# Opening of a transform-and-feed-forward kernel: one list of single steps over ten units, conversions in place on VectorE, a compact first-stage table

## The chip, the core and the metric

The kernel runs on one core of a Trainium2 chip. The engines are named as in the profile: PE (TensorE, matrix products), DVE (VectorE), ACT (ScalarE), POOL (GpSimd) and SP (SyncE, which here only issues DMAs). Each engine works through its own queue in order; semaphores order the engines among each other. The metric is the time of the program on the device in microseconds; less is better. The kernel before takes 1809.57 us, the median of three runs (1808.49 to 1812.95).

## The reference

```python
def _attn_ref(x):                         # x: 8 x 3072 x 256, float32
    X = np.fft.fft(x, axis=1)
    X = np.fft.fft(X, axis=2)
    return X.real.astype(np.float32)

def _moe_ref(x, w_in, w_out):             # x: the result above as 24576 x 256
    h = x @ w_in                          # w_in: 256 x 2048, float64
    g = np.maximum(h, 0.0) + np.log1p(np.exp(-np.abs(h)))
    return (g @ w_out).astype(np.float32) # w_out: 2048 x 256, float64
```

So: the real part of a two-dimensional Fourier transform of each of 8 batches, then a feed-forward network with softplus on each of the 24576 rows. [...]

## The kernel before

**The transform** along the sequence (3072 = 24 x 128) is made in two stages. Stage A multiplies with a table (`fe`, and `fo` that is made from it on ACT by `fo_prep`, L270) and writes its result `t_d` to memory; the host's arrangement of x allows two cheap folds (`fold_a`, `fold_b`, L168 and L173) ahead of it. A batch goes through stage A in four groups of 3 or 4 column sets. Stage B (`load_y`, `stage_b`, `stage_b_out`) reads rows of `t_d` back and multiplies with a cosine table `bc`. The transform along the 256 columns is not made on the data: its cosine table `cd` is multiplied into w_in once (`w1_prep`, L303). The data are split by symmetry, so that each output row and its mirror come from one sum and one difference.

**Blocks and units.** The rows are cut into 25 blocks (`BLOCKS`), three for each batch and four for the last, of up to 512 columns each. For every block the network runs in 8 units (`UB`), each 256 of the 2048 hidden columns; 200 units in all. A unit u has a first layer (`mm1`, L455: twelve products in two halves, P and Q, each half in one of the two PSUM slots `pq`), then on DVE two additions of an edge term to P (`pc`, L475), the sum and the difference with Q (`h`, L553 and L554), on ACT four softplus (`gh` rounded, `h` full, L574 and L575), on DVE the low parts (`gl` = full minus rounded, `low_part`, L514), and a second layer (`mm2`, L485: four times six products into two accumulators). The second layer of unit u - 2 (`LAG`) stands behind the first layer of unit u in PE's queue. Every operand of a product is kept as a rounded high part and a low part, and three products (high-high, high-low, low-high) make one. After 8 units the accumulators are copied out on ACT (`evac`, L507).

The edge term needs one row of a block on all partitions: ACT copies it (`er`, L263), SP stores it to `e_d` and loads it back to all partitions (`eb`).

**The weights.** w_in and w_out come in as eight chunks each of 128 x 512 float64 numbers. Chunk c of w_in is loaded (`load_wi`), converted to float32 by steps on bits (`to_f32_a`, `to_f32_b`: five on DVE, L278 to L292, one on ACT, L298, two on POOL, L299 and L300), multiplied with `cd` on PE (`w1_prep`, L307 and L316), rounded on ACT (L323), and its low part taken on DVE (`w1_lo`, L329). A chunk of w_out is converted in the same way, rounded on ACT (L340), and its low part is taken on POOL (L341). Unit u needs chunk u of both.

**The order.** `PLAN` is a table of tokens written out by hand. The entry `s` runs ahead of the units: it loads, makes batch 0's stage A and block 0's stage B, and converts chunks 0 to 5 of w_in and prepares w1 from 0 to 4 of them. The entries `0a`, `0b`, `0d` to `7d` run at three places inside units 0 to 7 and hold the rest of the conversions. Behind that a loop over units u hangs further work to fixed units (`tasks`): the loads, folds and stage A of the next batch, stage B of the next block. Each token and each loop body appends its instructions to the engines' queues in the order of the program. All loads and stores go through SP's queue. Raw chunks of weights lie in buffers that units use later (`gh`, `gl`, `xt`, `wr`).

## Time and profile before

| | us |
|---|---|
| median of three runs | 1809.57 |
| the profiled execution | 1808.19 |
| its span, first to last instruction | 1806.3 |
| PE busy in the span | 1750.1 |
| DVE busy | 1275.7 |
| ACT busy | 930.4 |
| POOL busy | 171.8 |
| mean granted clock of PE | 0.982 of full |

The page gives sums over the span; a question about one stretch of it needs the busy times by windows and the instructions in order of time. In a row of the latter stand the start, the length, the engine, the line of the kernel, the operation, what it writes and reads, the shape and how many instructions are merged; in square brackets follows how long the engine had been idle and what ended that. A float32 product counts as two instructions, a rounded one as one. In a row of waits stand who waited for whom, the total, how often, and the longest.

### The profile page before, as it was taken

Reading aid. Unit: us, or ns where it says so; the run is one execution under the profiler, and the core shown is the slowest. Engines: PE = TensorE matmul, PEld = TensorE weight load, DVE = VectorE, ACT = ScalarE, POOL = GpSimd, SP = SyncE. Lnnn points to the kernel's source line nnn. Section 1 sums busy time; section 2 is a strip of 40 time slices with the busy share of each in tenths; the row PEclk is TensorE's granted clock in tenths of the full one; section 3 lists DMA queues with packets and bytes.
Section 4 is the critical chain, followed back from the end, with each engine's and each line's share of the span. In section 5 each row is a group of like instructions: output and inputs, shape, how many; then the busy total and the mean of one; then the engine's idle time right before and its main releaser. Section 6 shows DMA issues by size and latency. Waiting matters only on the chain.

```text
span 1806.3 us, 20128 instructions
## 1 busy us (share of the span) xinstructions
PE 1750.1 (97%) x8196; PEld 1474.4 (82%) x8196; DVE 1275.7 (71%) x1337; ACT 930.4 (52%) x970; POOL 171.8 (10%) x156
## 2 busy tenths in 40 slices
PE   4589999999999999999999999999999999999999
PEld 4467888888888888888888888888888888899999
DVE  3599667677776677766776677766777667767775
ACT  1245555555555455555545545555555555555554
POOL 1245101110011001010010100110010200000000
PEclk7789999999999999999999999999999999999999
DMA  6302221310103102121012111131021210001000
GB/s 185 118 20 69 83 69 40 92 61 18 53 22 101 41 18 63 52 70 50 24 40 76 53 41 34 30 96 57 18 63 44 78 47 24 14 37 39 23 18 19
DMA packets 39339, 94.84 MB, mean 53 GB/s; under 512 B 2958, under 2 KB 18978, under 8 KB 38287
## 3 DMA queue, kind: packets, MB, share of 16 engines
q1 hardware_dynamic: 39247, 93.56, 17.6%
q8 instruction: 65, 1.06, 0.2%
q14 instruction: 27, 0.22, 0.0%
HBM read 55.00 MB, written 38.54 MB: 52 GB/s over the span
## 4 chain that ended last, share of the span: by engine, by line
PE 90%; ACT 0%; ACTq 0%; issue 0%
PE acc L495 57%; PE pq L466 28%; PE pq L223 1%; PE pq L183 1%; PE pq L184 1%; PE pq L225 1%; PE pq L230 0%; PE pq L227 0%; PE pq L236 0%; ACT o L507 0%; ACTq L615 0%; PE pq L244 0%; PE pq L247 0%
## 5 line engine op out<-in xcount | busy, mean ns | idle before, releaser
L495 PE MATMUL acc<-gh,wo 128*128 128x512 f32 (+2 forms) x3200 | 1016.5, 386 | 2.0 <-DVE wn L335 2.0
L495 PEld LDWEIGHTS acc<-gh,wo 128*128 128x128 f32 x3200 | 600.3, 188 | 117.4 <-ACT gh L574 2.4
L574 ACT ACTIVATE gh<-h 128x1024 fp32r<-128x1024 f32 (+2 forms) x400 | 407.1, 1018 | 476.5 <-DVE h L553 475.9
L495 PE MATMUL acc<-gl,wo 128*128 128x512 f32 (+2 forms) x1600 | 617.5, 386 | 0.0
L475 DVE SCALAR_TENSOR_TENSOR pc<-eb,wn,pq 128x512 f32<-128x512 f32 (+2 forms) x400 | 272.7, 723 | 442.0 <-PE pq L466 442.0
L466 PE MATMUL pq<-x,w 128*128 128x512 f32 (+5 forms) x2400 | 574.5, 388 | 4.9 <-DVE h L554 2.7
L466 PEld LDWEIGHTS pq<-x,w 128*128 128x128 f32 (+1 forms) x2400 | 449.8, 189 | 96.9 <-PE pq L466 4.5
L514 DVE TENSOR_TENSOR gl<-h,gh 128x1024 fp32r<-128x1024 f32 (+2 forms) x400 | 470.6, 1218 | 0.0
L575 ACT ACTIVATE h<-h 128x1024 f32<-128x1024 f32 (+2 forms) x400 | 411.0, 1028 | 12.7
L495 PEld LDWEIGHTS acc<-gl,wo 128*128 128x128 f32 x1600 | 301.9, 189 | 54.5
L553 DVE TENSOR_TENSOR h<-pq,pc 128x1024 f32<-128x1024 f32 (+2 forms) x200 | 236.6, 1183 | 21.8 <-DVE pc L475 1.4
L554 DVE SCALAR_TENSOR_TENSOR h<-pq,pc 128x1024 f32<-128x1024 f32 (+2 forms) x200 | 234.6, 1173 | 0.0
L170 POOL TENSOR_TENSOR xt<-xt 120x387 f32<-120x387 f32 (+1 forms) x28 | 26.2, 935 | 1149.0 <-DMA xt<-in_xh 1149.0
L192 ACT ACTIVATE st<-pq 125x768 f32<-125x768 f32 (+1 forms) x32 | 27.8, 867 | 133.3 <-PE pq L184 133.3
L260 ACT ACTIVATE x<-pq 128x1024 fp32r<-128x1024 f32 (+2 forms) x25 | 24.9, 994 | 135.1 <-PE pq L225 83.6
L183 PE MATMUL pq<-xt,fe 120*125 120x129 f32 x208 | 43.5, 293 | 17.3 <-DMA fe<-in_fe 11.9
L183 PEld LDWEIGHTS pq<-xt,fe 120*125 120x125 f32 x208 | 35.9, 204 | 20.5 <-issue 15.5
L507 ACT ACTIVATE o<-acc 128x1024 f32<-128x1024 f32 (+2 forms) x52 | 47.1, 956 | 7.7 <-PE acc L495 7.3
L307 PE MATMUL wps<-wt,cd 128*128 128x256 f32 x64 | 25.9, 576 | 24.4 <-POOL wt L300 24.4
L184 PE MATMUL pq<-xt,fo 120*125 120x127 f32 x208 | 43.2, 292 | 2.0 <-DVE xt L176 1.1
L307 PEld LDWEIGHTS wps<-wt,cd 128*128 128x128 f32 x64 | 18.1, 297 | 29.5 <-POOL wt L300 25.8
L223 PE MATMUL pq<-bc,y 128*128 128x128 f32 (+2 forms) x208 | 39.9, 273 | 1.4 <-DVE pc L475 1.4
(50 smaller groups left out, 454.5 us busy)
## 6 DMA issues: line engine op xcount, KB each, us to landing
...
```

Of the source, the lines that this page charges most:

```text
L183: nc.tensor.matmul(out=psv[0:YR, i, 127:D], lhsT=fe[:, g0 + i, :], rhs=t[:, i, 1, :], start=True, stop=True)
L184: nc.tensor.matmul(out=psv[0:YR, i, 0:127], lhsT=fo[:, g0 + i, :], rhs=t[:, i, 3, 2:NE], start=True, stop=True)
L223: nc.tensor.matmul(out=ps[:, 0, c : c + n], lhsT=y[0:kk, i, 128:256], rhs=cos, start=True, stop=True)
L466: nc.tensor.matmul(out=ps[:, g, 0:n], lhsT=w1[0 : 128 - t, t, a, f0 : f0 + 128], rhs=x1[0 : 128 - t, t, c, 0:n], start=(i == 0), stop=(i = ...
L475: nc.vector.scalar_tensor_tensor(out=pc[:, g, 0:n], in0=eb[:, 0:n], scalar=wn[:, 2 * fu + g : 2 * fu + g + 1], in1=p_ps[:, g, 0:n], op0=AL ...
L495: nc.tensor.matmul(out=acc[:, ec, 0:n], lhsT=wo[:, a, fc, ec * 128 : (ec + 1) * 128], rhs=src[:, sign, g, 0:n], start=(fu == 0 and g == 0 ...
L507: nc.scalar.activation(out=o[:, e0:e1, 0:n], in_=acc_t[sign][:, e0:e1, 0:n], func=AF.Copy)
L514: nc.vector.tensor_tensor(out=gl[:, sg, :, 0:n], in0=h_t[u][:, sg, :, 0:n], in1=gh_t[u][:, sg, :, 0:n].bitcast(F32), op=ALU.subtract,)
L553: nc.vector.tensor_tensor(out=h[:, 0, :, 0:n], in0=q_ps[:, :, 0:n], in1=pc[:, :, 0:n], op=ALU.add)
L554: nc.vector.scalar_tensor_tensor(out=h[:, 1, :, 0:n], in0=q_ps[:, :, 0:n], scalar=-1.0, in1=pc[:, :, 0:n], op0=ALU.mult, op1=ALU.add,)
L574: nc.scalar.activation(out=gh[:, sg, :, 0:n], in_=hv, func=AF.Softplus)
L575: nc.scalar.activation(out=hv, in_=hv, func=AF.Softplus)
```

## The change

The opening is rewritten. What it does:

- **One list.** The entry `s` and the entries of units 0 to 7 are replaced by one list of tokens, each a single step on one engine, which covers the loads, batch 0's stage A, the stage B of blocks 0 and 1, all conversions, and units 0 to 9 up to the second layer of unit 7. The loop starts at unit 10 (`N0`). Tokens of a unit: `MP`, `MQ` first layer; `pc`, `pd` edge terms; `hp`, `hm` sum and difference; `sa`, `sb` softplus; `gl` low part; `U7_01` a quarter of the second layer of unit 7. Of the weights: `C0A` to `C4G` and `K0A` to `K3G` steps of conversion of w_in and w_out, `P`, `Wh`, `wn`, `Wl` preparation of w1, `Oh`, `Ol` of wo.
- **Conversions.** Chunks 0 and 1 of w_in are converted alone, chunks 2 to 7 in pairs (1024 elements), and so are all of w_out. The steps A to F are on DVE, D and F write over the raw words; the last step G is on DVE for w_in and on POOL for w_out. ACT has no part in it.
- **Table.** The host gives a table with 25 entries per column set instead of 125 and five columns of 0 and 1; 20 copies on ACT with a scale per partition spread it into `fe` and `fo`. It takes 314,400 bytes instead of 780,000.
- **Order of loads; stores of stage A.** Group 2 of batch 0 comes first. The rows of `t_d` that block 0 needs are stored from ACT's queue at once (`T`), the rest from SP's queue later (`t`). All folds of batch 0 are on DVE.
- **w1 preparation** of chunks 4 to 7 uses the PSUM slots of the first layer. `wn` is copied on ACT.
- Named buffers replace the pools that turn; the work hung to units of the loop moves by a few units for batch 1 and blocks 2 and 3.

```diff
-PLAN = {
-    "s": (
-        "X0 I1 L0 I0 X1 X2 X3 I2 L1 F0f f0f I3 A0 a0 C0 D0s F1f f1f A1 a1 F2f f2f A2 a2 L2 P0 W0d F3f f3f "
-        "A3 a3 L3 C1 D1s Y0 L4 P1 W1d C2 D2s L5 C3 D3s L6 P2 W2d P3 W3d L7 B0 b0 C4 D4s M0 P4 W4d C5 D5s M1"
-    ),
-    "0a": "P5",
...
+N0 = 10
+CHUNKS = ((0,), (1,), (2, 3), (4, 5), (6, 7))
+PLAN = """
+Ife X2 Ibc X0 X1 X3 L0 L3 L2 Icd fex L1 fex2 F2 f2 A2 F0 a2 T2 f0 A0 F1 f1 a0 A1 F3 T0 a1 f3 T1 C0A A3 C0B
+C0C C0D a3 C0E C0F T3 C0G C2A C2B P0 C2C C2D C1A C1B Wh0 C1C wn0 C1D C1E Y0 C1F L4 L5 C1G M1 C2E M0 P1 C2F
+C2G B0 wn1 Wl0 Wh1 Wl1 P2 x1h0 x1l0 C3A MP0 er0 C3B wn2 Wh2 E0 C3C t0 MQ0 t2 Wl2 C3D P3 C3E Eb0 L6 C3F M2 t3
...
+    on = (jj[:, None] == np.arange(NJ)[None, :]).astype(float)
+    half = R // 2
+    ang = 2 * np.pi * ((s[:, :, None] * np.arange(half + 1)) % S) / S
+    cs, sn = np.cos(ang), np.sin(ang)[:, :, 1:]
+    fe = np.concatenate([cs, -sn], axis=2)
+    fo = np.concatenate([-cs[:, :, :1], -sn, -cs[:, :, 1:]], axis=2)
+    fx = np.concatenate([fe.reshape(XP, -1), fo.reshape(XP, -1), on], axis=1)
...
+    def stage_a_store(eng, b, gi, st, rows):
+        for r0, r1 in rows:
+            eng.dma_start(out=t_d[b, r0:r1, g0 : g0 + ng, :], in_=st[r0:r1])
...
+    def e_load(blk):
+        i, n = blk["i"], blk["n"]
+        eb = eb_t[i] = buf(f"eb{i % 2}", [128, 512])
+        nc.sync.dma_start(out=eb[:, 0:n], in_=e_d[i : i + 1, 0:n].to_broadcast([128, n]))
...
+    def spread(fx, g0, g1):
+        for k, f in enumerate((fe, fo)):
+            v = fx[:, k * NG * (R + 1) : (k + 1) * NG * (R + 1)].rearrange("p (g c) -> p g c", g=NG)
+            for j in range(NJ):
+                on = 2 * NG * (R + 1) + j
+                nc.scalar.activation(
+                    out=f[:, g0:g1, :, j], in_=v[:, g0:g1, :], func=AF.Copy, scale=fx[:, on : on + 1]
+                )
...
+    def to_f32(step, raw, p):
         lo, hi = raw[:, :, 0], raw[:, :, 1]
-        ti, pi = t.bitcast(I32), p.bitcast(I32)
-        nc.vector.tensor_scalar(
-            out=pi, in0=pi, scalar1=0x07FFFFFF, scalar2=3, op0=ALU.bitwise_and, op1=ALU.logical_shift_left
-        )
-        nc.vector.scalar_tensor_tensor(
...
+        elif step == "D":
+            v.scalar_tensor_tensor(
+                out=hi, in0=hi, scalar=-0x40000000, in1=pi, op0=ALU.bitwise_and, op1=ALU.bitwise_or
+            )
...
+        elif step == "F":
+            v.scalar_tensor_tensor(
+                out=lo.bitcast(F32), in0=lo.bitcast(U32), scalar=2.0**-52, in1=p, op0=ALU.mult, op1=ALU.mult
+            )
+
+    def to_f32_end(eng, raw, p):
+        eng.tensor_tensor(out=p, in0=raw[:, :, 1].bitcast(F32), in1=raw[:, :, 0].bitcast(F32), op=ALU.add)
 
...
+        ps = slot() if c >= 4 else pa.tile([128, 2, 512], F32, tag=f"acc{c % 2}", name="wps")
...
+        RAW_I, RAW_O = ("gl0", "gl1", "gh2", "xt"), ("wr", "gl2", "wr", "wr")
+        XTAG, STAG = ("xt", "h0", "h1", "x10"), ("os0", "os1", "os2", "h1")
+        FIRST, REST = ((5, 25), (65, 85)), ((0, 5), (25, 65), (85, YR))
...
+        def convert(key, step):
+            if key not in cvt:
+                if key[0] == "C":
+                    ch = CHUNKS[int(key[1])]
+                    raw = raws["i", ch[0] // 2]
+                    where = {1: ("pc", ch[0]), 2: ("x11", ch[0] // 2 - 1)}[len(ch)]
+                    if where[0] not in space:
+                        shape = [128, 2, 512] if where[0] == "pc" else [128, 2, 1024]
+                        space[where[0]] = buf(where[0], shape)
+                    p = space[where[0]][:, where[1] % 2]
+                    r = raw[:, ch[0] % 2 : ch[-1] % 2 + 1].rearrange("p c f t -> p (c f) t")
+                    for j, c in enumerate(ch):
+                        lone[c] = p[:, j * 512 : (j + 1) * 512]
+                else:
+                    k = int(key[1])
+                    r = raws["o", k].rearrange("p c f t -> p (c f) t")
+                    p = osbuf(k % 2)[:, 0:1024]
+                cvt[key] = r, p
+            r, p = cvt[key]
+            if step == "G":
+                to_f32_end(nc.gpsimd if key[0] == "K" else nc.vector, r, p)
+            else:
+                to_f32(step, r, p)
+
+        def do(tok):
...
+            elif k == "T":
+                stage_a_store(nc.scalar, 0, c, hold["st", c], FIRST)
+            elif k == "t":
+                stage_a_store(nc.sync, 0, c, hold["st", c], REST)
...
+            elif k == "er":
+                hold["e", c] = e_copy(BLOCKS[c], hold["b", c], buf("eb1", [128, 512]) if c == 0 else osbuf(2))
...
+            elif k in ("Oh", "Ol"):
+                hi, lo = (wo[:, i, 4 * c : 4 * c + 4, :] for i in range(2))
+                tv = cvt[f"K{c}"][1].rearrange("p (c e) -> p c e", e=D)
+                if k == "Oh":
+                    nc.scalar.activation(out=hi, in_=tv, func=AF.Copy)
+                else:
+                    nc.gpsimd.tensor_tensor(out=lo, in0=tv, in1=hi.bitcast(F32), op=ALU.subtract)
+            elif k in ("MP", "MQ"):
+                mm1(c, int(k == "MQ"))
+            elif k in ("pc", "pd"):
+                p_out(c, int(k == "pd"))
+            elif k in ("hp", "hm"):
+                h_out(c, int(k == "hm"))
+            elif k in ("sa", "sb", "gl"):
+                (soft_hi, soft, low_part)[("sa", "sb", "gl").index(k)](a[1], a[0])
+            elif k == "U":
+                mm2(c, a[1] // 10, a[1] % 10)
...
+        for tok in PLAN.split():
+            do(tok)
+        evac(0, 0)
...
+            u0 = first[b - 1] * UB + (N0 if b == 1 else 0)
+            for gi in range(4):
+                hang(u0 + 2 * gi, ("x", b, gi))
+                hang(u0 + 2 * gi + 2, ("a", b, gi))
+        for i in range(2, len(BLOCKS)):
+            u0 = (i - 1) * UB
+            hang(u0 + (2 if i > first[B - 1] else 6 if i == 3 else 3), ("b", i))
+            hang(N0 if i == 2 else u0 - 3 if i > 3 else u0 + 4, ("y", i))
...
+        for u in range(N0, NU + LAG):
...
```

The order on the engines, first before, then after. DVE, from the low part of block 0 (`x`, L261 before and L276 after) on. Before (`wt`, `wir` are a chunk of w_in in conversion, `w_81` is w1):

```order
L261 TENSOR_TENSOR x_265<-pq,x_265 128x2x512
L278 TENSOR_SCALAR wt<-wir 128x512
L281 TENSOR_SCALAR wt<-wt 128x512
L286 TENSOR_SCALAR wt<-wt 128x512
L289 SCALAR_TENSOR_TENSOR wt<-wir,wt 128x512
L292 TENSOR_SCALAR wt<-wt 128x512
L329 TENSOR_TENSOR w_81<-wps,w_81 128x2x256
L335 COPY wn<-wps 128x2
```

After (`gh`, `wr` hold raw words of w_in and w_out, `x` and `os` the space of the conversion):

```order
L276 TENSOR_TENSOR x<-pq,x 128x2x512
L309 TENSOR_SCALAR x<-gh 128x1024
L311 TENSOR_SCALAR x<-x 128x1024
L313 TENSOR_SCALAR x<-x 128x1024
L548 TENSOR_TENSOR w_75<-wps,w_75 128x2x256
L317 SCALAR_TENSOR_TENSOR gh<-gh,x 128x1024
L321 TENSOR_SCALAR x<-gh 128x1024
L323 SCALAR_TENSOR_TENSOR gh<-gh,x 128x1024
L309 TENSOR_SCALAR os<-wr 128x1024
```

A chunk's conversion and the low part of the same chunk, which stood one behind the other, are apart now: between the steps of one pair stands the low part of another chunk, and a pair of w_out follows ahead of unit 0.

PE, from the preparation of chunk 4 of w1 before, and of chunk 2 after. Before (L307 and L316 prepare w1, L466 is the first layer):

```order
L307 MATMUL wps<-wt,cd 128x256 x4
L316 MATMUL wps<-cd,wt 128x1 x4
L466 MATMUL pq<-x_265,w_81 128x512 x12
L307 MATMUL wps<-wt,cd 128x256 x4
L316 MATMUL wps<-cd,wt 128x1 x4
L466 MATMUL pq<-x_265,w_81 128x512 x12
```

After (L334 and L343 prepare w1, L372 is the first layer, L436 the second):

```order
L334 MATMUL wps<-x,cd 128x256 x4
L343 MATMUL wps<-cd,x 128x1 x4
L372 MATMUL pq<-x,w_75 128x512 x12
L334 MATMUL wps<-x,cd 128x256 x4
L343 MATMUL wps<-cd,x 128x1 x4
L372 MATMUL pq<-x,w_75 128x512 x18
L436 MATMUL acc_369<-gh,wo 128x512
```

Five chunks were prepared ahead of unit 0's first layer, now three; unit 1 and half of unit 2 follow chunk 3 at once, and the second layer of unit 0 ahead of the other half.

SP, from the last loads of w_in ahead of block 0's edge row on. Before (`e_d`, `eb` the edge row, `wor` w_out):

```order
L358 DMA wir<-in_w_in 128x2x512 x4
L266 DMA e_d<-er 1x512
L267 DMA eb<-e_d 128x512
L367 DMA wor<-in_w_out 128x2x512 x3
L204 DMA y<-t_d 65x4x256
```

After (`t_d<-os` are the stores of stage A that block 0 does not need):

```order
L467 DMA gh<-in_w_in 128x2x512 x2
L467 DMA wr<-in_w_out 128x2x512 x2
L287 DMA e_d<-eb 1x512
L204 DMA t_d<-os 5x1024
L204 DMA t_d<-os 40x1024 x2
L204 DMA t_d<-os 5x768
L204 DMA t_d<-os 40x768 x2
L292 DMA eb<-e_d 128x512
```

Loads of w_out have moved ahead of the edge row, and six stores stand between its store and its load.

More of the change, by code (lines that the diff above doesn't have):

```diff
@@ L136, in tile_fft2_softplus_ffn @@
 @with_exitstack
-def tile_fft2_softplus_ffn(ctx: ExitStack, tc: tile.TileContext, xh, w_in, w_out, fe_d, cd_d, bc_d, out):
+def tile_fft2_softplus_ffn(ctx: ExitStack, tc: tile.TileContext, xh, w_in, w_out, fx_d, cd_d, bc_d, out):
     nc = tc.nc
@@ L200, in load_y @@
         t = t_rows(b)
[L201 removed]
+        y = buf("y", [128, 5, D])
         ks = [k for k, _, _ in blk["cols"] if k]
@@ L534, in tile_fft2_softplus_ffn @@
             pst = {}
-            for tok in PLAN.get(f"{u}a", "").split():
-                do(tok)
             for t in todo:
```

450 lines of the change are left out of this document (210 added, 240 removed).

## Prediction

> **What bounds the kernel now.** I read the busy times of the page first, then the busy times in three stretches of the opening, then TensorE (PE) and VectorE (DVE) in order of time.
>
> ```profile
> span 1806.3 us, 20128 instructions
> PE 1750.1 (97%) x8196; PEld 1474.4 (82%) x8196; DVE 1275.7 (71%) x1337; ACT 930.4 (52%) x970; POOL 171.8 (10%) x156
> ```
> ```profile
> 0.00:85.00 85.00, 43.27 (x177) 37.28 (x178) 35.19 (x61) 14.80 (x22) 16.12 (x16) 0.74 0.57 161
> 85.00:183.00 98.00, 87.63 (x348) 68.78 (x348) 95.12 (x111) 53.56 (x63) 45.87 (x32) 0.89 0.15 41
> 183.00:199.70 16.70, 16.70 (x92) 14.15 (x91) 10.91 (x11) 7.62 (x8) 3.40 (x4) 1.00 0.46 139
> ```
>
> The columns are length, then PE, PE's weight loads, DVE, ACT and POOL busy, the granted clock, the DMA share and GB/s. Of the 56.2 us in which PE is idle (1806.3 - 1750.1), 52.1 lie before 183 us (183 - 43.3 - 87.6), and the last 4 are the end of the output. From 183 us on PE never pauses, at full clock. Only the opening has room, and there the limit changes: up to 85 us neither engine is full (DVE 35.2 of 85), from 85 to 183 DVE is (95.1 of 98).
>
> ```profile
> 72.59 3.05 PE L466 MATMUL pq<-x,w 128*128 128x512 f32 x12
> ...
> 183.02 2.96 PE L466 MATMUL pq<-x,w 128*128 128x512 f32 x12
> ```
> ```profile
> 61.70 1.22 DVE L261 TENSOR_TENSOR x<-pq,x 128x1024 fp32r<-128x1024 f32 x1 [1.56 <-ACT x L260]
> ```
>
> Counting first layers from 72.59 (unit 0), the one at 183.02 is unit 10. By then units 0 to 9 have had their first layer and 0 to 7 their second, and this is just what the new list of steps holds. I call this moment T10. Behind it lie 1806.3 - 183.0 = 1623.3 us of PE work without a pause, which the change leaves as they are (the loop's moved loads have several units to land). So the prediction is a prediction of T10. The L261 row is the second mark: block 0 is ready for the units at 62.9, and T10 comes 120 us later.
>
> ```profile
> DVE w L329 <- ACT w L323: 35.1, 6, 10.2
> ```
>
> Why 62.9: a chunk of w_in goes from DVE over ACT, POOL, PE and ACT back to DVE, with all else behind it in DVE's queue. DVE stood 35.1 us for the end of this round trip.
>
> **The change, term by term. Term 1, block 0 ready.**
>
> ```profile
> 0.00:10.00 10.00, 0.00 (x0) 0.00 (x0) 1.90 (x3) 1.28 (x1) 0.20 (x4) 1.00 0.82 185
> 10.00:20.00 10.00, 4.60 (x18) 3.84 (x18) 5.60 (x11) 3.35 (x5) 1.30 (x1) 1.00 0.98 247
> ```
> ```profile
> 55.94 1.99 PE L307 MATMUL wps<-wt,cd 128*128 128x256 f32 x8
> 57.77 0.95 PE L316 MATMUL wps<-cd,wt 128*128 128x1 f32 x8
> 58.58 0.47 PE L223 MATMUL pq<-bc,y 128*128 128x128 f32 x2
> ...
> 60.22 0.39 PE L225 MATMUL pq<-bc,y 128*128 128x128 f32 x2
> ...
> 79.43 3.78 PE L307 MATMUL wps<-wt,cd 128*128 128x256 f32 x8 [3.79 <-POOL wt L300]
> 83.01 1.71 PE L316 MATMUL wps<-cd,wt 128*128 128x1 f32 x8
> 84.57 4.99 PE L466 MATMUL pq<-x,w 128*128 128x512 f32 x12
> ```
> ```profile
> 13.86 0.43 DVE L286 TENSOR_SCALAR wt<-wt 128x512 int32<-128x512 int32 x1
> 14.33 0.69 DVE L289 SCALAR_TENSOR_TENSOR wt<-wir,wt 128x512 int32<-128x512 int32 x1
> 15.05 0.43 DVE L292 TENSOR_SCALAR wt<-wt 128x512 int32<-128x512 int32 x1
> ```
>
> DVE's second chunk (C1) needs the eleventh load; ahead of it and with it stand 6.0 MB (table 0.31, x 3.22, cosines 0.39, four w_in chunks 2.10). The first 10 us move 1.85 MB, later ones 0.247 a us: 26.8, and with 2 for landing 29. The compact table saves 0.47 MB (2 us) and costs 20 short ACT copies instead of 3; these lie beside the loads of x. C1's seven steps on 512 elements take 0.47 each for four one-input steps and 0.72 for three two-input ones (start to start in these rows), 4.0: 33. Steps D and F now write in place over every second word, which no row shows; between 0.43 and 1.4 (twice its row) I take the 0.69 of L289, which already reads every second word. P1, the product that prepares C1's part of w1, at half clock takes 5.1 (79.43 to 84.57; at full clock 2.6, from 55.94 to 58.58): 38.1; block 0's transform 2.0 (58.58 to 60.61): 40.1; its high part on ACT some 1.2 and its low part 1.2: 42.5. I take **43**, 20 earlier than before. The stores of the first stage, whose first rows go ahead on ACT's queue, must be in memory by about 33.
>
> **Term 2, DVE from there to the low part of unit 1.**
>
> ```profile
> 76.52 1.40 DVE L475 SCALAR_TENSOR_TENSOR pc<-eb,wn,pq 128x512 f32<-128x512 f32 x2
> 78.03 1.23 DVE L553 TENSOR_TENSOR h<-pq,pc 128x1024 f32<-128x1024 f32 x1
> 79.17 1.22 DVE L554 SCALAR_TENSOR_TENSOR h<-pq,pc 128x1024 f32<-128x1024 f32 x1
> ...
> 148.50 2.35 DVE L514 TENSOR_TENSOR gl<-h,gh 128x1024 fp32r<-128x1024 f32 x2
> ```
>
> Start to start: the two halves of P 1.5, each h 1.14, two low parts 2.27, a w1 low part, half an h step, 0.62. A 1024-element conversion exists nowhere in the trace. A two-input step should take 1.25, as h does; a one-input step lies between 0.47 (no dearer than 512 elements) and 0.94 (two of them). I take 0.73, nearer to two since the work doubles. Six steps A to F are then 4 x 0.73 + 2 x 1.25 = 5.4. In the new order stand: three such conversions (C3, K0, K1) 16.3; the C3 end step 1.1; pc and pd of units 0, 1, 2: 4.5; five h steps 5.7; four low parts 4.5; two w1 low parts 1.2. Sum **33.4**; PE then stands at 43 + 33.4 = 76.4. Going on, DVE has 64.5 more to the last h of unit 9 (K2, K3, C4 17.3, seven units' pc and pd 10.5, fifteen h steps 17.1, fourteen low parts 15.9, four w1 low parts 2.5, block 1's 1.2), so 140.9 if it never waits.
>
> **Term 3, PE from there to T10.** Now PE has more left than DVE. A first layer is 2.78 (12 products of the pitch of 0.2315 in the 5.54 us groups below), a second 5.56, a w1 preparation 2.64, a block transform 2.0, as above. Left: half of unit 1's second layer 2.8, six more 33.3, thirteen first-layer halves 18.1, four preparations 10.6, block 1 2.0: **66.8**, so 143.2.
>
> ```profile
> 216.69 5.54 PE acc L495 x24
> ```
>
> **Term 4, handing over to the loop.**
>
> ```profile
> 183.66 1.94 ACT L507 ACTIVATE o<-acc 128x1024 f32<-128x1024 f32 x2
> ```
>
> Before, the first accumulator was copied out (0.97) under unit 10's first layer. Now the DVE queue ends close to T10, so two softplus copies (2.1) and this copy come late, of which half a first layer covers 1.4: **2**. Together 145.
>
> **Costs that no row gives.** (a) POOL keeps eight operations of 1024 elements, about 2.5 each (twice a 512 row).
>
> ```profile
> 49.13 1.40 DVE L281 TENSOR_SCALAR wt<-wt 128x512 f32<-128x512 f32 x1
> ...
> 146.23 1.23 DVE L553 TENSOR_TENSOR h<-pq,pc 128x1024 f32<-128x1024 f32 x1
> ```
> ```profile
> 48.89 1.35 POOL L299 TENSOR_TENSOR wt<-wir,wt 128x512 f32<-128x512 f32 x1 [9.33 <-issue]
> ...
> 146.35 1.29 POOL L300 TENSOR_TENSOR wt<-wt 128x512 f32<-128x512 f32 x1
> ```
>
> A one-input step beside POOL took 1.40 (0.43 alone), while an h step, which reads PSUM, lost nothing. So 0 to 20; most of the eight stand beside pc, pd and h: 3. (b) Cold clock on PE: after an idle 3.8 PE ran at half speed for 10 us (79.43 to 89.6, a preparation and a first layer of 5.0 where the one at 72.59 took 3.05). PE will idle about 5 us before unit 1's first layer; from 0 (the cold stretch ends while PE still waits for DVE) to 10: 4. (c) PE and DVE waiting for each other in a fixed order: 0 to 10; DVE lost 3% from 85 to 183, so 3 of 100. With these T10 = **155**, 28 earlier. The profiled execution took 1808.19, 1.9 over its span and 1.4 under the median of 1809.57: 1623.3 + 155 + 1.9 = **1780**.
>
> **Rivals.** (1) *Waits in SP's queue.* Block 0's edge row, the remaining stores of the first stage and the loads of w_out stand in one row, each behind semaphores of earlier transfers and of POOL; K0 and K1 write over buffers that those stores still read.
>
> ```profile
> 36.34 0.25 SPq L193 DMA_DIRECT2D t_d<-st  x1
> ...
> 43.04 0.32 SPq L204 DMA_DIRECT2D y<-t_d  x1
> ```
>
> A store took 6.7 us until the load behind it could go. By my sums K0 has some 1 us of room and K1 2; if each of these places loses 5 to 7, T10 is 165 to 175: 1790 to 1800. For it: everything is tight there; against it: each store is now split over few rows. (2) *Block 0 is no earlier than before* (the change doesn't do what it says): 62.9 + 33.4 + 66.8 + 2 + 10 = 175, 1800. It needs Y0 or P1 20 us late; DMA at 0.57 of its share up to 85 us speaks against it. (3) *Slower: PE stays at half clock.* After 43 PE has 90 of work (six preparations 15.8, ten first layers 27.8, eight second 44.4, block 1 2.0). At half speed all along T10 is 43 + 180 = 223: 1848. It decides where over 53% of this work, (183 - 43 - 2) / 90 - 1, is cold and nothing else waits. For it the 10 us above; against it the clock of 0.89 between 85 and 183, when PE paused more often. The Trainium skill, page "TensorE: Matmul & The Clock Gate", section "What's actually happening", says that the clock is full after one busy window of some 3.4 us; by it this rival would have no chance. The rows from 79.43 on disagree, with 10 us of unbroken work at half speed, so I leave it a small one. (4) *Only the sums count*: without (a) to (c) T10 is 145 or a little less, 1767 to 1770.
>
> **How the numbers follow.** Forecast 0.66 (T10 147 to 165, 1772 to 1790), rival 1 0.16, rival 2 0.08, rival 3 0.04, rival 4 0.06. The range leaves out rivals 2 and 3, the upper third of 1 and part of 4: 1767 to 1797. A measurement of this kernel can tell about 0.3%, 5.4 us, from no change: faster means under 1804. All but rival 3 lie there by their middles; I give 0.05 to no change, for rivals 1 and 2 with (a) near its upper end: 0.91, 0.05, 0.04.
>
> **What would show it.** Right: block 0's low part on DVE ends at 40 to 46; DVE is over 90% busy from 43 to 140; PE over 90% from 80 on; unit 10's first layer starts at 147 to 165; the rest stays 1623. Wrong: DVE waits of several us named after a DMA (rival 1), L261's successor after 55 (rival 2), a clock under 0.7 after 80 us (rival 3), DVE steps of 1.4 to 3 us beside POOL (a). A pause of PE after T10 would break the whole sum.

## The result and the profile after

| | before | after |
|---|---|---|
| median, four runs each | 1809.03 | 1782.37 (1780.08 to 1784.40) |
| ratio, 95% interval | | 0.9848 (0.9829 to 0.9867) |
| the profiled execution, its span | 1808.19, 1806.3 | 1781.84, 1780.1 |
| block 0's low part done | 62.9 | 43.9 |
| T10, start of unit 10 | 183.0 | 145.7 |
| from T10 to the end of the span | 1623.3 | 1634.4 |

The forecast was 1780, and the time lies 2.4 us from it. But its two halves were both wrong: T10 came 9.3 us before the 155 forecast, ahead even of the 147 to 165 that the prediction gave as its sign of being right, and what follows T10 took 11.1 us more than the 1623.3 that were to stay. That the sum came out is luck.

The page after, its first two lines, and the busy times in four stretches (columns as before: length, PE, weight loads, DVE, ACT, POOL, clock, DMA share, GB/s):

```profile
span 1780.1 us, 20092 instructions
PE 1744.8 (98%) x8196; PEld 1466.8 (82%) x8196; DVE 1265.5 (71%) x1308; ACT 927.3 (52%) x975; POOL 130.9 (7%) x124
```
```profile
0.00:43.90 43.90, 25.42 (x116) 23.04 (x116) 24.98 (x41) 14.52 (x30) 0.20 (x4) 0.88 0.74 209
43.90:78.70 34.80, 24.92 (x99) 19.17 (x100) 32.69 (x38) 13.61 (x17) 7.58 (x4) 0.85 0.48 146
78.70:145.70 67.00, 66.57 (x314) 54.93 (x313) 62.09 (x66) 33.56 (x39) 10.85 (x5) 1.00 0.06 20
145.70:158.27 12.57, 10.18 (x38) 7.57 (x36) 8.33 (x9) 10.19 (x10) 0.00 (x0) 0.86 0.48 125
```

From block 0 on, DVE is the full engine (32.69 of 34.80), and from 78.7 to T10 it is PE (66.57 of 67.00, at full clock). Then, in the stretch that should be the seamless start of the loop, PE is idle for 2.4 us and its clock is 0.86.

In order of time, the marks of the prediction: block 0's low part and `gl1_1` (the low part of unit 1's second half) on DVE, the one DVE step that POOL visibly held up (0.69 alone), and PE around T10.

```profile
42.69 1.23 DVE L276 TENSOR_TENSOR x<-pq,x 128x1024 fp32r<-128x1024 f32 x1 [3.29 <-ACT x L272]
...
77.06 1.22 DVE L419 TENSOR_TENSOR gl<-h,gh 128x1024 fp32r<-128x1024 f32 x1
...
95.15 2.87 DVE L309 TENSOR_SCALAR x<-xt 128x1024 int32<-128x1024 int32 x1
```
```profile
94.66 2.82 POOL L557 TENSOR_TENSOR wo<-os,wo 128x1024 fp32r<-128x1024 f32 x1 [2.37 <-ACT wo L555]
```
```profile
145.69 1.56 PE L372 MATMUL pq<-x,w 128*128 128x512 f32 x6
148.15 1.64 PE L372 MATMUL pq<-x,w 127*128 127x512 f32 x6 [0.90 <-DVE h L402]
151.29 0.79 PE L436 MATMUL acc<-gh,wo 128*128 128x512 f32 x1 [1.50 <-ACT os L448]
...
158.27 2.96 PE L372 MATMUL pq<-x,w 128*128 128x512 f32 x12
```

The first product at 151.29 lasts 0.79 instead of 0.39: a stretch at half clock, 150.7 to 154.1 in the trace's clock record, costs another 1.7.

The rest of the 11.1 is spread over the whole loop. First layers of units 55, 56 and 57, before and after, and one of unit 170 in each:

```profile
586.44 2.96 PE L466 MATMUL pq<-x,w 128*128 128x512 f32 x12
594.77 2.96 PE L466 MATMUL pq<-x,w 128*128 128x512 f32 x12
604.44 2.96 PE L466 MATMUL pq<-x,w 128*128 128x512 f32 x12
```
```profile
554.99 2.94 PE L372 MATMUL pq<-x,w 128*128 128x512 f32 x12
563.39 2.96 PE L372 MATMUL pq<-x,w 128*128 128x512 f32 x12
573.07 2.95 PE L372 MATMUL pq<-x,w 128*128 128x512 f32 x12
```
```profile
1596.65 2.27 PE L466 MATMUL pq<-x,w 128*128 128x384 f32 x12
```
```profile
1569.35 2.28 PE L372 MATMUL pq<-x,w 128*128 128x384 f32 x12
```

Unit 55 takes 8.33 before and 8.40 after. The lead over the kernel before falls from 32.4 us at unit 26 to 31.4 at unit 56 and 27.3 at unit 170: **5.1 us lost in a stretch in which neither kernel's PE ever waits** and the program is the same. Every third unit loses 0.07, the others 0.02. The second layer alone, from the chain that ended last, before (the row of 5.54 us in the prediction) and after (first unit 11, one of the units that lose 0.07, then one of the others):

```profile
182.43 5.61 PE acc L436 x24
...
539.90 5.55 PE acc L436 x24
```

So the 11.1 are 2.4 idle, 1.7 and 1.7 of clock (the second time from 1679.9 to 1683.3), and the drift of 5.1; 10.9 in sum. (The lead falls by 4.9 from unit 10 to unit 26, 0.8 more than pauses and clock, and behind unit 170, where the blocks are narrower, the drift gives some 0.5 back.) The drift was the one thing with no place in the prediction.

### The profile page after: what moved, and what is told of

Same layout as the page of the kernel before. It is cut to its first block, busy times and chain, and to the rows that moved or that the text cites. A ratio compares the mean times of both kernels' runs of the same rounds, so it can differ in the third digit from the quotient of the medians.

```text
span 1780.1 us, 20092 instructions
## 1 busy us (share of the span) xinstructions
PE 1744.8 (98%) x8196; PEld 1466.8 (82%) x8196; DVE 1265.5 (71%) x1308; ACT 927.3 (52%) x975; POOL 130.9 (7%) x124
## 4 chain that ended last, share of the span: by engine, by line
PE 94%; DVE 3%; DMA 1%; issue 1%; ACT 0%; SPq 0%; ACTq 0%; DVEq 0%
PE acc L436 59%; PE pq L372 30%; PE pq L234 1%; PE pq L236 1%; PE pq L191 1%; PE pq L192 1%; DMA x<-in_xh 1%; DVE gl L419 1%; DVE h L400 0%; DVE h L402 0%; DVE pc L385 0%; DVE gl L317 0%; PE wps L334 0%; ACT gh L408 0%; PE pq L241 0%
## 5 line engine op out<-in xcount | busy, mean ns | idle before, releaser
L436 PE MATMUL acc<-gh,wo 128*128 128x512 f32 (+2 forms) x3200 | 1023.2, 388 | 1.5 <-ACT os L448 1.5
L436 PEld LDWEIGHTS acc<-gh,wo 128*128 128x128 f32 x3200 | 600.4, 189 | 119.7 <-ACT os L448 1.9
L436 PE MATMUL acc<-gl,wo 128*128 128x512 f32 (+2 forms) x1600 | 617.7, 386 | 1.5 <-DVE gl L419 1.5
L372 PE MATMUL pq<-x,w 128*128 128x512 f32 (+5 forms) x2400 | 572.6, 387 | 9.4 <-DVE pc L385 6.8
L372 PEld LDWEIGHTS pq<-x,w 128*128 128x128 f32 (+1 forms) x2400 | 448.3, 189 | 100.4 <-DVE pc L385 7.2
L419 DVE TENSOR_TENSOR gl<-h,gh 128x1024 fp32r<-128x1024 f32 (+2 forms) x400 | 465.7, 1204 | 1.3 <-ACT h L413 1.3
L436 PEld LDWEIGHTS acc<-gl,wo 128*128 128x128 f32 x1600 | 302.1, 189 | 59.7 <-DVE gl L419 2.4
L198 ACT ACTIVATE os<-pq 125x768 f32<-125x768 f32 (+1 forms) x31 | 26.9, 868 | 126.1 <-PE pq L192 126.1
L448 ACT ACTIVATE os<-acc 128x1024 f32<-128x1024 f32 (+2 forms) x52 | 47.0, 954 | 7.8 <-PE acc L436 7.3
L191 PE MATMUL pq<-xt,fe 120*125 120x129 f32 x190 | 37.6, 280 | 0.6 <-DVE xt L181 0.6
L236 PE MATMUL pq<-bc,y 128*128 128x128 f32 x192 | 38.1, 281 | 0.0
L192 PE MATMUL pq<-xt,fo 120*125 120x127 f32 x190 | 37.3, 279 | 0.0
L234 PEld LDWEIGHTS pq<-bc,y 128*128 128x128 f32 (+1 forms) x208 | 34.2, 196 | 2.1 <-issue 0.3
L276 DVE TENSOR_TENSOR x<-pq,x 128x1024 fp32r<-128x1024 f32 (+2 forms) x25 | 29.4, 1176 | 8.0 <-ACT x L272 8.0
```

The costliest lines, as they stand in the source:

```text
L191: nc.tensor.matmul(out=psv[0:YR, i, 127:D], lhsT=le, rhs=t[:, i, 1, :], start=True, stop=True)
L192: nc.tensor.matmul(out=psv[0:YR, i, 0:127], lhsT=lo, rhs=t[:, i, 3, 2:NE], start=True, stop=True)
L234: nc.tensor.matmul(out=ps[:, 0, c : c + n], lhsT=y[0:kk, i, 128:256], rhs=cos, start=True, stop=True)
L236: nc.tensor.matmul(out=ps[:, 1, c : c + n], lhsT=y[:, i, 0:128], rhs=cos, start=True, stop=True)
L372: nc.tensor.matmul(out=ps[:, g, 0:n], lhsT=w1[0 : 128 - t, t, a, f0 : f0 + 128], rhs=x1[0 : 128 - t, t, c, 0:n], start=(i == 0), stop=(i = ...
L419: nc.vector.tensor_tensor(out=gl_t[u][:, sg, :, 0:n], in0=h_t[u][:, sg, :, 0:n], in1=gh_t[u][:, sg, :, 0:n].bitcast(F32), op=ALU.subtract,)
```

## The experiments

All times are from one profiled execution, the medians from the timed runs (the kernel before beside them: 1808.0 to 1809.7). "Rest" is the span from T10 on. Pitch is the time from the start of one product to the start of the next. A set is one of the three pairs of buffers `gh` and `gl` that the units use in turn; set 2 is `gh2` and `gl2`.

| kernel | median | ratio to before | block 0 | T10 | rest |
|---|---|---|---|---|---|
| after | 1782.37 | 0.9848 (0.9829 to 0.9867) | 43.9 | 145.7 | 1634.4 |
| e1_layout | 1775.97 | 0.9816 (0.9797 to 0.9835) | 44.3 | 146.1 | 1630.6 |
| e2_aligned | 1771.29 | 0.9788 (0.9772 to 0.9804) | 41.7 | 143.3 | 1623.9 |
| e7_handover | 1778.53 | 0.9834 (0.9812 to 0.9855) | 42.3 | 143.4 | 1631.3 |
| e6_warm | 1782.06 | 0.9850 (0.9828 to 0.9873) | 44.5 | 145.2 | 1635.1 |
| e4_before_dve | 1805.47 | 0.9977 (0.9967 to 0.9987) | 59.1 | 180.8 | 1623.3 |
| e3_roundtrip | 1786.74 | 0.9869 (0.9841 to 0.9898) | 47.2 | 148.0 | 1634.5 |
| e10_stores | 1788.34 | 0.9878 (0.9854 to 0.9903) | 49.6 | 151.2 | 1635.8 |
| e5_fulltable | 1782.49 | 0.9846 (0.9822 to 0.9871) | 44.7 | 145.9 | 1634.3 |
| e8_all192 | 1758.38 | 0.9722 (0.9702 to 0.9742) | 41.6 | 143.1 | 1613.1 |
| e9_best | 1749.52 | 0.9675 (0.9661 to 0.9688) | 41.4 | 142.3 | 1604.4 |

### The drift: where the operands lie

**e1_layout** asks for all buffers once, in the order in which the kernel before had them, so that each gets its old address:

```diff
+    for tag, n in (("xt", 2064), ("y", 1280), ("pc", 1024), ("wr", 2048), ("h0", 2048), ("h1", 2048), ("x10", 2048),
+                   ("x11", 2048), ("eb0", 512), ("eb1", 512), ("gh0", 2048), ("gh1", 2048), ("gh2", 2048),
+                   ("os0", 1032), ("os1", 1032), ("os2", 1032), ("gl0", 2048), ("gl1", 2048), ("gl2", 2048)):
+        buf(tag, [128, n])
```

> The changed kernel with every named SBUF buffer at the address that the buffer of the same use had before (gh0 to gh2 at 160768 to 177152, gl0 to gl2 at 197728 to 214112, x1, h, pc, y, os likewise); no instruction moves. Theory 'place': the 5 us by which the loop after unit 10 runs slower than before (the start of unit 170 is 27.3 us earlier than before, that of unit 10 37.3; one unit in three, whose second layer reads gh2 and gl2, takes 0.07 us more, the others 0.02) comes from where the buffers of the second layer lie; the third set's mean pitch falls from 228.4 ns to about 225, the drift goes from unit 26 on, unit 10 stays at 145.7, and the time is 5 us lower, about 1777. Rival 'order': the drift comes from what the loop's engines do beside PE (the offset of 10 units, the loads of x and y hung elsewhere); the pitch stays at 228.4 for one unit in three and the time at 1782.

(The pitches in the expectations are means of the steps between starts that take in the narrower blocks of the last batch. Over blocks of 512 columns alone, 228.4 is 234.2, 225 to 226.5 is 231 to 232, and 222.7 is 227.8.)

The first layers of units 55 and 56:

```profile
555.22 2.96 PE L377 MATMUL pq<-x,w 128*128 128x512 f32 x12
563.55 2.96 PE L377 MATMUL pq<-x,w 128*128 128x512 f32 x12
```

Unit 55 takes 8.33 again, the pitch of every set is back at that of before (230.97 to 230.99), and from unit 34 to unit 170 the kernel takes 1195.86 us, to the hundredth what the kernel before takes (after: 1200.80). T10 stands. The rest falls by 3.8 only, because the stretch at half clock at the hand-over lasts 6.8 us in this execution (151.0 to 157.8) and not 3.4. The whole drift is the place of the buffers: the new named buffers are laid out in order of first use, and no one had chosen an address.

**e2_aligned** tries an alignment of 64 bytes.

```diff
-        return buf(f"os{k}", [128, 1032])
+        return buf(f"os{k}", [128, 1040])
...
```

> The changed kernel with the three os buffers 4160 instead of 4128 bytes wide, so that everything behind them moves by 32 to 96 bytes and every buffer of the loop starts at a multiple of 64 bytes; before, gh0 to gh2 did and gl0 to gl2 were 32 off; in the changed kernel gh0 to gh2 are 32 off, gl0 and gl1 are not, gl2 is, and the slow set is the one where both are off. Theory 'alignment': the slow third goes, pitch 225 in all three sets or a little less than before, time about 1777 or 1776. Rival 'place': the buffers lie where they lay but for 96 bytes, so the third set keeps its 228.4 ns and the time stays at 1782. Rival 'order': stays too.

Set 2 fell from 234.2 to 227.8 ns, below anything in the kernel before, and the first layer of odd blocks (which reads `x11`) from 232.8 to 230.2; sets 0 and 1 (gh now a multiple of 64, gl as it was) kept their 232. So a place can be better than before, but it isn't the multiple of 64 that counts. The median fell by 11 us beside the changed kernel.

**m1_pitch** measures the cost by itself: 24 products of the second layer's form for each of twelve sets of places, with PE alone and beside ACT and DVE.

```diff
+        for phase in range(4):
...
+            for k, (w, a, b) in enumerate(CASES):
+                w, a, b = w // 4, a // 4, b // 4
+                for i in range(24):
+                    f = w + 128 * (i % 12)
+                    r = mw[:, b : b + 512] if i % 3 == 1 else mv[:, a + 512 * (i // 12) : a + 512 * (i // 12) + 512]
+                    nc.tensor.matmul(out=ps[:, i // 12, :], lhsT=wt[:, f : f + 128], rhs=r, start=True, stop=True)
```

> Only products of the second layer's form (128x128 weights, 512 columns, operands in the order a, b, a), 24 for each of twelve sets of places (weights, a, b as bytes behind a multiple of 1024), in four phases: PE alone, with ACT copying 1024 elements without pause, with VectorE subtracting without pause, with both; nothing of the reference is computed. Theory 'PE itself': the pitch depends on the places in the first phase already, about 222.7 ns with both operands at 192 and 225 to 228 elsewhere, and by the same amounts in all phases. Theory 'contention': in the first phase all places give one pitch (within 0.5 ns), and the differences of 3 to 6 ns appear with ACT, VectorE or both. Rival: neither, one pitch within 0.5 ns in each phase; then what differs is something that this kernel lacks.

Windows over the twelve sets, PE alone, beside ACT, beside DVE (columns as above):

```profile
17.53:84.30 66.77, 66.77 (x290) 54.12 (x289) 0.00 (x0) 0.00 (x0) 0.00 (x0) 1.00 0.00 0
89.74:156.50 66.76, 66.76 (x289) 53.90 (x287) 0.00 (x0) 64.55 (x61) 0.00 (x0) 1.00 0.00 1
176.88:243.60 66.72, 66.72 (x289) 54.08 (x288) 64.74 (x53) 0.00 (x0) 0.00 (x0) 1.00 0.00 1
```

PE takes the same time in all three, whether ACT and DVE work without pause or not, and each set of places has its own pitch, equal to 0.05 ns in the three phases (in the fourth too, but for its first set, which fell on a pause): from 227.3 ns (weights 448, operands 192, 192) to 234.2 (448, 96, 96). So the differences are there with PE alone, and contention with ACT or DVE is not their cause.

**e8_all192** puts every buffer where the quick set of e2_aligned lay, and has the copy of e7_handover (below). The diff is against e1_layout.

```diff
-    for tag, n in (("xt", 2064), ("y", 1280), ("pc", 1024), ("wr", 2048), ("h0", 2048), ("h1", 2048), ("x10", 2048),
+    for tag, n in (("xt", 2064), ("gap", 48), ("y", 1280), ("pc", 1024), ("wr", 2048), ("h0", 2048), ("h1", 2048), ("x10", 2048),
...
-                   ("os0", 1032), ("os1", 1032), ("os2", 1032), ("gl0", 2048), ("gl1", 2048), ("gl2", 2048)):
+                   ("os0", 1056), ("os1", 1056), ("os2", 1056), ("gap2", 160), ("gl0", 2048), ("gl1", 2048), ("gl2", 2048)):
```

> The changed kernel with the earlier copy of the first accumulator (of e7_handover) and all buffers of both layers (x1, gh, gl, also h and pc) 192 bytes behind a multiple of 1024, where the quickest set of e2_aligned lay (222.69 ns; its first layer on odd blocks 222.72). Theory 'the place within 1024 bytes decides': all three sets and both halves of the first layer near 222.7; 24 x 4.0 + 12 x 3.3 ns less in each of 190 units, 26 us, time about 1752. Rival 'what else is read and written at the time decides': sets 0 and 1 keep their 225 to 226.5 and even blocks their 226.4; time 1766 to 1772 (1771 of e2_aligned less the 3 of the hand-over, and some).

1758.4: between the two, nearer to the theory. The second layer's chain piece is 5.49, and all three sets are alike (228.5).

**m2_places** looks for the rule behind it.

```diff
+CASES = (
+    [(w, a, a) for w in (384, 448) for a in range(0, 1024, 32)]
+    + [(w, 192, 192) for w in range(0, 512, 32)]
+    + [(448, 192, b) for b in range(0, 1024, 64)]
+)
```

> PE alone, as in the first phase of m1_pitch, over 96 sets of places: both operands together at every 32 bytes of 1024 with the weights at 384 (as w1) and at 448 (as wo); the weights at every 32 bytes of 512 with both operands at 192; the second operand at every 64 bytes with the first at 192. Theory 'period': the pitch repeats with a short period in the operands' place (128, 256 or 512 bytes), and 192 of m1_pitch (227.3 ns with the weights at 448) is among the lowest; m1_pitch had 64 at 233.1, so not 128. Rival 'no period': the pitch wanders between 227 and 235 ns without an order that a rule could be made of; then only trying helps. Nothing of the reference is computed.

The pitch in ns, from the starts of 24 products each, by the operands' place within 256 bytes (columns 0, 32, 64 to 224; values of the second to the fourth period, which agree to 0.1, the first differs by up to 0.8):

```
weights at 384 (128 within 256):  233.5  234.0  233.5  233.1  227.7  233.4  229.3  233.9
weights at 448 (192 within 256):  229.3  233.9  233.5  234.0  233.5  233.1  227.7  233.4
```

The period is 256 bytes, and the two rows are one, shifted by 64: what counts is **how far the operands lie from the weights**. At the same place within 256 bytes 227.7, 64 behind 229.3, elsewhere 233 to 234. When only the weights move, the same pattern comes (226.7 against 229.3 to 233.9); when the two operands lie apart, 228.4 becomes 229.5 to 233.5. (The same set of places, weights at 448 and both operands at 192, stands here as 227.7, 226.7 and 228.4: its first products depend on what ran before, as e9_best will show.) With this the kernels can be read: w1 lies at 128 and wo at 192; before, x1 lay at 0, gh at 0 and gl at 96; in the changed kernel gh at 96 and gl at 0, 0 and 96, the last set with nothing at 64 behind.

**e9_best** keeps gh and gl at 192 and moves x1 from 192 to 128, with a `gap3` of 48 elements ahead of `x10` and this one behind `eb1` (the diff is against e8_all192):

```diff
...
-                   ("x11", 2048), ("eb0", 512), ("eb1", 512), ("gh0", 2048), ("gh1", 2048), ("gh2", 2048),
+                   ("x11", 2048), ("eb0", 512), ("eb1", 512), ("gap4", 16), ("gh0", 2048), ("gh1", 2048), ("gh2", 2048),
```

> As e8_all192, but each operand at the same place within 256 bytes as its weights: x1 at 128 (w1 lies at 128; in e8_all192 x1 lay 64 behind it), gh and gl at 192 (as wo, unchanged). Theory of m2_places (period 256; 227.7 ns at the same place, 229.3 at 64 behind, 233 to 234 elsewhere): the first layer's products lose up to 1.6 ns each, 12 a unit, 3.6 us over 190 units, the second layer is unchanged: 1754 to 1756 against 1758.4. Rival: 192 within 1024 was the good place for its own sake, and the first layer gets slower by up to 6 ns a product, 14 us: 1772.

Units 55 and 56, and a second layer from the chain that ended last:

```profile
541.06 2.92 PE L377 MATMUL pq<-x,w 128*128 128x512 f32 x12
549.26 2.92 PE L377 MATMUL pq<-x,w 128*128 128x512 f32 x12
```
```profile
175.44 5.44 PE acc L441 x24
```

A unit takes 8.20 (8.40 after), a second layer 5.44. The median is 1749.5, 9 us better than e8_all192 where 2 to 4 were expected, and not where they were: the first layer's mean pitch stays at 230.2, while the second layer, whose buffers kept their place within 256 bytes, falls to 227.0. So the rule of m2_places doesn't price the first layer, which should have come to 227.7. Product by product, in e8_all192 some nine products behind the first layer run unevenly (224 to 236) before they settle at 227; in e9_best all but the first of the second layer are at 227. So the place of the first layer's operands also disturbs the products after it. The record of m2_places has the same: its products at weights 448, operands 192 begin with five uneven ones behind a set with operands at 160, with nine behind one whose second operand lay at 128, and with none where only the weights had changed. Why this is so, no run here shows. This is the best version of the study, 33 us under the changed kernel by the medians, 3 of them from the hand-over.

### The parts of T10

**e7_handover** copies the first accumulator out ahead of unit 9's softplus:

```diff
-U7_01 hm8 sa0_8 U7_10 pc9 sb0_8 pd9 MQ9 sa1_8 gl0_8 sb1_8 U7_11 hp9 gl1_8 sa0_9 hm9 sb0_9 sa1_9 sb1_9
+U7_01 hm8 sa0_8 U7_10 pc9 sb0_8 pd9 MQ9 sa1_8 gl0_8 sb1_8 V U7_11 hp9 gl1_8 sa0_9 hm9 sb0_9 sa1_9 sb1_9
...
+            elif k == "V":
+                evac(0, 0)
...
-        evac(0, 0)
```

> The changed kernel with the copy of the first accumulator moved in ACT's queue from the end of the list to ahead of the last four softplus copies of unit 9 (behind sb1_8). Theory 'hand-over' (term 4): PE's wait of 1.50 us ahead of unit 8's second layer at 151.3 goes, and the stretch of half clock from 150.7 to 154.1 that follows the pauses (1.7 us) may go with it: 1.5 to 3.2 us, time 1779 to 1780.5. Rival: ACT is itself on the path (the softplus copies of unit 9 come 1 us later, and PE waits for them at unit 11 or 9's second layer): 0 to 0.5 us, time 1782.

```profile
145.88 1.64 PE L372 MATMUL pq<-x,w 127*128 127x512 f32 x6 [0.90 <-DVE h L402]
147.36 0.39 PE L436 MATMUL acc<-gh,wo 128*128 128x512 f32 x1
...
152.97 0.40 PE L372 MATMUL pq<-x,w 128*128 128x512 f32 x1
```

The 1.50 is gone, and with it the stretch at half clock: from unit 10 to unit 11 it takes 9.5 (143.4 to 153.0) instead of 12.6. Term 4 with what it triggers is worth 3.0.

The half clock is not the only price, though. In e3, e5, e6 and e10, which keep the late copy and its pause of 1.50, no stretch at half clock fell here; there PE waits 0.8 to 1.8 us in unit 11 for the load of block 2. In e5_fulltable, and then that load in SP's queue, after and in e7_handover:

```profile
162.33 0.46 PE L234 MATMUL pq<-bc,y 128*128 128x128 f32 x2 [0.81 <-DMA y<-t_d]
```
```profile
152.14 0.73 SPq L215 DMA_DIRECT2D y<-t_d  x1
```
```profile
143.31 0.73 SPq L215 DMA_DIRECT2D y<-t_d  x1
```

The load stands behind the store of the first accumulator, so the early copy lets it go 9 us earlier too. From unit 10 to unit 13 these four take 33.4 to 34.5 us, the changed kernel 33.8 and e7_handover 30.6: the late copy costs some 3, through one or the other.

**e6_warm** fills PE's pause before unit 1 with products of no use (`Z`, which stands behind `P3` in the list):

```diff
...
+            elif k == "Z":
+                z = pa.tile([128, 2, 512], F32, tag="acc0", name="z")
+                for i in range(26):
+                    nc.tensor.matmul(
+                        out=z[:, i % 2, :], lhsT=w1[:, 0, 0, 0:128], rhs=x1_t[0][:, 0, 0, :], start=True, stop=True
+                    )
```

> The changed kernel with 26 products without use (w1 by block 0, into the first accumulator, which is free there; 6.0 us at full clock) behind the preparation of chunk 3, in PE's pause from 49.5 to 56.4. Unit 1's first layer and what follows then start at full clock: its 18 products that took 6.98 us take 4.2. Theory 'DVE sets the time up to 78': PE only waits longer for DVE (the waits of 1.56, 0.72, 0.76 up to 78.3 grow by the 2.8), gl1_1 ends at 78.3 less at most 1.1 (the two DVE waits of 0.56 and 0.55 on pq go), and T10 is 0 to 1.1 earlier. Rival, the term (b) on record: cold PE costs T10 4 us, and T10 comes 3 to 4 us earlier, time 1778 to 1779.

First the changed kernel's row, then those of e6_warm:

```profile
56.37 6.98 PE L372 MATMUL pq<-x,w 128*128 128x512 f32 x18 [6.84 <-DVE pc L385]
```
```profile
49.98 6.29 PE L569 MATMUL z<-x,w 128*128 128x512 f32 x26
56.95 1.66 PE L372 MATMUL pq<-x,w 128*128 128x512 f32 x6 [0.68 <-DVE pc L385]
59.50 3.13 PE L372 MATMUL pq<-x,w 127*128 127x512 f32 x12 [0.89 <-DVE h L402]
```

The clock stays full (six products in 1.66 and twelve in 3.13, where eighteen took 6.98), but PE only waits for DVE instead. `gl1_1` starts at 76.54 against 77.06, with block 0 ready 0.6 later: 1.1 at most, not the 4 of term (b).

**e3_roundtrip** and **e4_before_dve** take order and conversions apart. The first has the new order with the old round trip, the second the old order with all steps on DVE.

```diff
-            v.scalar_tensor_tensor(
-                out=lo.bitcast(F32), in0=lo.bitcast(U32), scalar=2.0**-52, in1=p, op0=ALU.mult, op1=ALU.mult
-            )
+            nc.scalar.activation(out=lo.bitcast(F32), in_=lo.bitcast(U32), func=AF.Copy, scale=2.0**-52)
+            nc.gpsimd.tensor_tensor(out=lo.bitcast(F32), in0=lo.bitcast(F32), in1=p, op=ALU.mult)
...
-            to_f32_end(nc.gpsimd if key[0] == "K" else nc.vector, r, p)
+            to_f32_end(nc.gpsimd, r, p)
```
```diff
-            nc.scalar.activation(out=lo.bitcast(F32), in_=lo.bitcast(U32), func=AF.Copy, scale=2.0**-52)
-            nc.gpsimd.tensor_tensor(out=p, in0=lo.bitcast(F32), in1=p, op=ALU.mult)
-        nc.gpsimd.tensor_tensor(out=t, in0=t, in1=p, op=ALU.add)
+            nc.vector.scalar_tensor_tensor(
+                out=p, in0=lo.bitcast(U32), scalar=2.0**-52, in1=p, op0=ALU.mult, op1=ALU.mult
+            )
+        nc.vector.tensor_tensor(out=t, in0=t, in1=p, op=ALU.add)
```

> The changed kernel with its order, table and buffers, but with the last two steps of every conversion on ACT and POOL again (product by 2^-52 on ACT, product and sum on POOL): the order alone. Theory 'the order carries the gain, but it is written for the short conversion': DVE loses some 15 us of work up to unit 10, each chunk of w_in gets a round trip of 3 to 6 us instead of 1.4 to 2.5, and in a fixed order DVE waits for some of them: block 0's low part at 45 to 50 (43.9), unit 10's first layer at 147 to 160 (145.7 in the changed kernel), time 1783 to 1796. Rival 'the conversions carry it': unit 10 at 170 or later, time 1806 or more.

> The kernel before, with its own order of work, its full table and its buffers, but with the last two steps of every conversion on VectorE (the product by 2^-52 and the sum, that were on ACT and POOL): the conversions alone. Theory 'the order carries the gain': block 0's low part comes 10 to 18 us earlier (before 62.9), as the 35.1 us that DVE stands for the round trip shrink, but DVE, busy 95.1 of 98 us from 85 to 183, gets 16 times 1.4 = 22 us more work, half of it behind 85, so unit 10's first layer comes only 5 to 15 us earlier than 183: time 1794 to 1804. Rival 'the conversions carry it': unit 10 at 158 or earlier, time 1784 or less.

Unit 10, with the order alone and with the conversions alone:

```profile
147.99 1.56 PE L371 MATMUL pq<-x,w 128*128 128x512 f32 x6
```
```profile
180.75 2.96 PE L467 MATMUL pq<-x,w 128*128 128x512 f32 x12
```

With the order alone T10 is at 148.0: 35.0 of the 37.3 us. With the conversions alone it is at 180.8: 2.3, less than either theory said. DVE's waits for the rounding of w1, in e4_before_dve and after (35.1 us before):

```profile
DVE w L330 <- ACT w L324: 22.7, 5, 6.9
```
```profile
DVE w L548 <- ACT w L544: 2.3, 1, 2.3
```

In the old order a chunk's low part stands in DVE's queue right behind its conversion, so DVE waits for PE and ACT even when the conversion is its own; in the new order other work stands between. Of the 12.4 that e4_before_dve saved in that wait, DVE's added work took most back: its busy time up to T10 went from 130.3 (35.2 + 95.1 in the prediction) to 139.2. The table, the split stores and the buffers are in e3_roundtrip too, so its 35 us are those of order, table and stores together; the next run puts some 5.5 of them to the stores.

**e10_stores** undoes the split of the first stage's stores and moves them from ACT's queue back to SP's.

```diff
-                stage_a_store(nc.scalar, 0, c, hold["st", c], FIRST)
+                stage_a_store(nc.sync, 0, c, hold["st", c], ((0, YR),))
...
-                stage_a_store(nc.sync, 0, c, hold["st", c], REST)
+                pass
```

> The changed kernel with the stores of batch 0's first stage whole again and on SP's queue (four stores of all 125 rows where each was: first rows on ACT's queue, the rest later on SP's). Rival 1 on record was that SP's queue sets the time. Theory: a whole store keeps the queue from the loads of w_in and of block 0 behind it for some us, block 0's low part comes 3 to 7 us later (47 to 51) and unit 10's first layer with it (149 to 153), time 1785 to 1790. Rival: the stores are hidden, since DVE has chunk 2 and 3 to convert: 0 to 1 us.

SP's queue when it loads block 0, after and in e10_stores, and PE in the latter:

```profile
26.78 0.35 SPq L215 DMA_DIRECT2D y<-t_d  x1
```
```profile
37.96 0.32 SPq L215 DMA_DIRECT2D y<-t_d  x1
...
43.57 0.77 PE L234 MATMUL pq<-bc,y 128*128 128x128 f32 x2 [6.44 <-DMA y<-t_d]
```

The load is issued 11 us later, PE stands 6.4 for it, and T10 comes 5.5 later. So a store in SP's queue does hold up the load behind it, as rival 1 said, though at block 0's load and not at the edge row and w_out, where rival 1 looked for it. What splitting the stores and what the second queue is worth, this run does not tell apart.

**e5_fulltable** loads the full table and makes `fo` of it with three ACT copies.

```diff
-                hold["fx"] = buf("y", [128, 1280])[0:XP, 0 : 2 * NG * (R + 1) + NJ]
-                nc.sync.dma_start(out=hold["fx"], in_=fx_d)
+                nc.sync.dma_start(out=fe.rearrange("p g c j -> p g (c j)"), in_=fx_d)
...
+                    nc.scalar.activation(out=fo[:, :, 0:1], in_=fe[:, :, 0:1], func=AF.Copy, scale=-1.0)
+                    nc.scalar.activation(out=fo[:, :, 1 : 1 + h], in_=fe[:, :, 1 + h :], func=AF.Copy)
+                    nc.scalar.activation(out=fo[:, :, 1 + h :], in_=fe[:, :, 1 : 1 + h], func=AF.Copy, scale=-1.0)
```

> The changed kernel with the full table of the first stage (780 KB loaded, the second table made of it by three ACT copies) in place of the compact one (0.31 MB, 20 short ACT copies). On record: the compact table saves 0.47 MB of loads ahead of block 0, 2 us. Theory: block 0's low part and unit 10 come 2 us later than in the changed kernel (45.9 and 147.7), time 1784. Rival: nothing, since the 20 copies on ACT (4.7 to 11.6 us) delay the first product of the first stage by as much as the larger load: 0 to 0.5 us.

Chunk 1's conversion starts at 31.59 instead of 28.65, 2.9 later. But the stretch of half clock lies elsewhere (29.6 to 39.8, in the changed kernel 31.2 to 41.5), so block 0's transform falls behind it; its first products after, and in e5_fulltable:

```profile
37.83 0.78 PE L234 MATMUL pq<-bc,y 128*128 128x128 f32 x2
```
```profile
40.31 0.47 PE L234 MATMUL pq<-bc,y 128*128 128x128 f32 x2
```

T10 is 0.2 later. That lies within what executions of an unchanged opening differ by (block 0 at 41.4 to 44.5 in the changed kernel and its variants, and it goes with the half-clock stretches), so one execution can't price the table at T10; both theories stand.

## Why the prediction came out right, step by step

- **Term 1** held: block 0 ready at 43.9 (43 forecast). Conversion steps of 1024 elements take 0.69 and 1.23 (0.73 and 1.25 start to start, the values taken). The 2 us for the table are 2.9 where the loads end, and unproven at T10. What the split stores are worth (5.5) was not priced; it stood in the term as a condition only.
- **Term 2** held: `gl1_1` ends at 78.3, 34.4 behind block 0 for 33.4.
- **Term 3** held: 67.4 from there to T10 for 66.8, with PE full.
- **Term 4** was 2; the waits are 0.9 and 1.5, with 1.7 of clock after them, and all of it falls behind T10's mark and not ahead of it. So 2 us of each of the two errors are the same term on the other side of the mark.
- **The unknown costs** were the step that failed on the early side: "(a) 3, (b) 4, (c) 3", 10 us. (a) came once (2.2, on a stretch where PE set the time), (b) is 1.1 at most, and that is the 1.0 by which term 2 ran over: DVE waited 0.56 and 0.55 for unit 1's cold products, and e6_warm has neither wait. For (c) the 0.6 of term 3 is left. They were added as if each lay on the path; but up to 78 DVE sets the time and hides PE's cold clock, and behind it PE does and hides DVE's delays. T10 was that of rival 4, 145.
- **"1623.3 us of PE work without a pause, which the change leaves as they are"** is the step that failed on the late side, by 11.1: same instructions, but other addresses (5.1, shown by e1_layout), a hand-over that lies behind T10 (2.4) and two stretches of clock (3.4). So the sum was right by luck, because two errors of 9.3 and 11.1 cancel. Rival 4's time did not follow from its T10, and the sign that "would break the whole sum", a pause of PE after T10, did come (0.9 and 1.5).
- **Rival 1** did not come: from 43.9 to T10 no step of DVE waits for a DMA. **Rival 2** did not come either (43.9). **Rival 3**: the clock is 1.00 from 70 us to T10. The stretch at half clock from 51.7 to 61.9 lasts, though PE works from 56.4 on, over 5 us of unbroken work. The Trainium skill, page "TensorE: Matmul & The Clock Gate", section "What's actually happening", lets a busy window of some 3.4 us suffice, and the window runs free, it does not begin with the work. The trace agrees: its clock changes only on a grid of 3.41 us, whose points lie here at 51.7, 55.1, 58.5 and 61.9, and the window from 58.5 is the first that PE works through. In the rows of the prediction the points lie at 78.6, 82.0, 85.4 and 88.9, and PE works from 79.4; full clock came at 88.9, one window later than the rule has it, but in the window from 82.0 to 85.4 PE spent 1.7 us on products of one column (L316). Whether these count as work, no run tests. So those rows spoke less for rival 3 than the prediction took them to.
